# First entry of a fused attention and two-layer kernel: maxima and sums taken by TensorE, fewer whole products, another planned order

## The chip, the cores and the metric

One core of a Trainium2 chip runs one program. The metric is device time in microseconds (us). Three runs of the kernel before gave a median of 721.77 us, from 721.12 to 722.47 us. One more execution was profiled. Its engines are TensorE (PE for products and PEld for loads of the stationary operand), VectorE (DVE), ScalarE (ACT), GpSimd (POOL) and SyncE (SP), whose queue issues almost all transfers.

## What is computed

An attention between tokens and states runs first, and its rows then go through two feed-forward layers with different activations.

```python
def _attn_ref(x, state):                 # x (4, 8, 512, 64), state (4, 8, 32, 64)
    scores = scale * np.matmul(x, state.transpose(0, 1, 3, 2))
    scores = scores - scores.max(-1, keepdims=True)
    a = np.exp(scores)
    a /= a.sum(-1, keepdims=True) + 1e-09
    xread = np.matmul(a, state)          # tokens read states
    ...                                  # sread: states read tokens, the same way
    return np.concatenate([xread, sread], axis=2)

def _moe_ref(x, w_in, w_out):            # (2176, 512) -> 2048 -> 512
    h = x @ w_in
    g = np.where(h > 0.0, h, np.exp(np.minimum(h, 0.0)) - 1.0)
    return g @ w_out
def _moe2_ref(x, w_in, w_out):           # the same with h * tanh(log1p(exp(h)))
    ...
```

All inputs of the attention are float32, the weights float64 (read as pairs of 32-bit words and turned into float32 by ACT and DVE).

## The kernel before

**Blocks and steps.** The tokens of one batch entry are a block of 512 (blocks 0 to 3), and the 128 state rows are a small block of their own. The token part never forms `xread`: for each block the states are multiplied into the first weights (`fold`, PE line L574, result `m`), so that the first product of a step, `mm1`, is `m` times the probabilities `x`. The first layer is a list of steps (block, chunk j of 128 hidden columns): `mm1` gives `h`, `hidden` makes `g` from it on ACT and DVE (exp L806, relu L807, DVE L811 or L814), and two steps later `mm2` adds `g` times a row chunk of `w_out` into four accumulators (`acc`). Block 0 runs its chunks 0 to 7 first, then block 1 its chunks 0 to 7, then the second halves of both, then blocks 2 and 3.

**Whole and split products.** Most products are split: an operand is a high and a low part in the rounded type fp32r (copy on ACT, difference on DVE), and one product is three matmuls of 512 columns (L848, L849, L850). A whole product is one float32 matmul, which the trace shows as two records (L782 for `h`, L841 for `acc`). `whole_out` makes the second products of block 0 whole for chunks below `WHOLE_OUT = 6`; their `g` isn't split (L811), and the weight is split only after the step.

**First entry.** Block 0's probabilities are made at the program's start by `token_reads`, for two halves of four heads (`hf` 0 and 1). The x tiles are turned on PE (L641), scores come from 16 products on 64x32 pieces of the array (L653) with the states on partitions; then DVE turns each 32x32 square (L660) so that tokens are on partitions, takes the maximum over 32 states (L671), subtracts it (L672), ACT takes exp (L674), DVE sums (L675), adds eps (L676), takes the reciprocal (L677), multiplies (L678) and turns back (L680) into `x`. Ahead of that PE does ten turns of the identity (`warm`, L370), which wait until DVE has made it. The states of all four entries are loaded by two transfers of ACT's queue (L398).

**What sets the order.** Every operation is put into a `Plan` with a cost, its tiles and a due time, worked back from a table of step times; `run` is a list scheduler that takes, again and again, the operation that can start first (then the one due first) on any engine, and writes the instructions in that order. Each engine then executes its own list strictly in order. The two PSUM banks with the tag `att` are shared by folds, turns, scores and state reads.

## Time and profile before

| | |
|---|---|
| median of 3 runs | 721.77 us (721.12 to 722.47) |
| profiled execution, its own time | 722.41 us |
| its span, first to last instruction | 720.5 us |
| PE busy | 701.7 us, 97% of the span |
| DVE busy | 556.7 us, 77% |
| ACT busy | 495.8 us, 69% |
| granted TensorE clock, mean | 0.993 |

Busy time of PE counts overlapping records once, and a matmul's record reaches past the start of the next one; so the start-to-start spacing of records, and not their length, is what a product costs in a full stream. [...] A line number is that of the kernel before unless another is said.

### The profile page before, as it was taken

What the parts mean: (1) busy time and instruction counts of PE and PEld (TensorE: products, weight loads), DVE (VectorE), ACT (ScalarE), POOL (GpSimd) and SP (SyncE); (2) the same over time, 40 slices, a digit from 0 to 9 for tenths busy, and PEclk for the clock granted to TensorE, in tenths of its full rate; (3) what the DMA queues carried; (4) which work ended last, traced back from release to release, by engine and by line L of the source; (5) the groups of instructions that cost most, each with busy time, mean ns of one, the idle gap of its engine ahead of it and who ended that gap; (6) DMA issues with size and microseconds to landing.
All of it is one profiled execution on the core that took longest, in us unless ns stands there. A gap on an engine that the chain in (4) does not pass through costs nothing.

```text
span 720.5 us, 10191 instructions
## 1 busy us (share of the span) xinstructions
PE 701.7 (97%) x3698; PEld 546.3 (76%) x3698; DVE 556.7 (77%) x949; ACT 495.8 (69%) x861; POOL 3.0 (0%) x14
## 2 busy tenths in 40 slices
PE   5899999999989999999999999999999999999997
PEld 3345777777757778978887888878888888888886
DVE  6899988869879985447889998769738887767622
ACT  4797999768778776467868786669347666666522
POOL 0000000000000000000000000000000000000000
PEclk9799999999999999999999999999999999999999
DMA  9965556773685647106486454642035444401001
GB/s 224 276 180 138 128 174 227 234 234 99 209 258 167 200 146 246 51 20 229 164 279 225 150 147 127 221 163 58 1 117 147 136 127 125 142 27 58 15 1 58
DMA packets 65717, 106.83 MB, mean 148 GB/s; under 512 B 6660, under 2 KB 45572, under 8 KB 65668
## 3 DMA queue, kind: packets, MB, share of 16 engines
q1 hardware_dynamic: 63444, 105.53, 47.8%
q10 hardware_dynamic: 2224, 0.66, 0.4%
q8 instruction: 29, 0.48, 0.3%
q14 instruction: 20, 0.16, 0.1%
HBM read 78.38 MB, written 27.79 MB: 147 GB/s over the span
## 4 chain that ended last, share of the span: by engine, by line
PE 90%; DVE 7%; ACT 1%; issue 0%; DVEq 0%; ACTq 0%
PE prod L1018 20%; PE acc_acc L848 7%; PE acc_acc L850 7%; PE acc_acc L849 7%; PE accB L1057 4%; PE accB L1059 4%; PE accB L1058 4%; PE accA L1057 4%; PE accA L1059 4%; PE accA L1058 4%; PE h L791 3%; PE h L793 3%; PE h L792 3%; PE fold L574 2%; PE h L772 2%; PE acc_acc L841 2%
## 5 line engine op out<-in xcount | busy, mean ns | idle before, releaser
L1018 PE MATMUL prod<-x_t,pair 128*128 128x512 f32 x384 | 96.9, 390 | 0.5 <-ACT u__0_1_832_3916 L1044 0.5
L848 PE MATMUL acc_acc<-g,w_out 128*128 128x512 f32 x232 | 93.1, 401 | 0.0
L850 PE MATMUL acc_acc<-g,w_out 128*128 128x512 f32 x232 | 90.5, 390 | 0.0
L849 PE MATMUL acc_acc<-g,w_out 128*128 128x512 f32 x232 | 90.4, 390 | 0.0
L1018 PEld LDWEIGHTS prod<-x_t,pair 128*128 128x128 f32 x384 | 71.6, 188 | 15.5 <-ACT u__0_1_832_3916 L1044 1.0
L1018 PE MATMUL prod<-x_b,pair 128*128 128x512 f32 x288 | 72.4, 389 | 0.0
L976 ACT ACTIVATE e<-u,two 128x512 f32<-128x512 f32 x68 | 48.7, 722 | 21.7 <-DVE u L975 21.6
L1018 PEld LDWEIGHTS prod<-x_b,pair 128*128 128x128 f32 x288 | 54.1, 188 | 11.2
L814 DVE SCALAR_TENSOR_TENSOR e<-e,h 128x512 f32<-128x512 f32 x62 | 42.3, 683 | 25.5 <-ACT e L807 25.0
L806 ACT ACTIVATE e<-h 128x512 f32<-128x512 f32 x68 | 40.3, 595 | 26.2 <-PE h L793 17.3
L848 PEld LDWEIGHTS acc_acc<-g,w_out 128*128 128x128 f32 x232 | 43.7, 188 | 16.2 <-issue 5.4
L817 ACT CAST g<-e 128x512 fp32r<-128x512 f32 x62 | 38.4, 621 | 25.5 <-PE acc_acc L850 19.8
L978 DVE TENSOR_TENSOR u<-u,e 128x512 f32<-128x512 f32 x68 | 46.2, 687 | 12.0 <-ACT e L977 11.8
L818 DVE TENSOR_TENSOR g<-e,g 128x512 fp32r<-128x512 f32 x62 | 42.4, 685 | 14.6 <-ACT g L817 14.0
L850 PEld LDWEIGHTS acc_acc<-g,w_out 128*128 128x128 f32 x232 | 43.5, 188 | 9.3
L807 ACT ACTIVATE e<-e,one 128x512 f32<-128x512 f32 x68 | 49.2, 725 | 1.5
L1057 PE MATMUL accB<-w_out,g 128*128 128x512 f32 x128 | 50.0, 390 | 0.0
L849 PEld LDWEIGHTS acc_acc<-g,w_out 128*128 128x128 f32 x232 | 43.6, 188 | 8.4
L1059 PE MATMUL accB<-w_out,g 128*128 128x512 f32 x128 | 49.9, 390 | 0.0
L1058 PE MATMUL accA<-w_out,g 128*128 128x512 f32 x128 | 49.8, 389 | 0.0
L1059 PE MATMUL accA<-w_out,g 128*128 128x512 f32 x128 | 49.8, 389 | 0.0
L1058 PE MATMUL accB<-w_out,g 128*128 128x512 f32 x128 | 49.8, 389 | 0.0
(300 smaller groups left out, 1472.5 us busy)
## 6 DMA issues: line engine op xcount, KB each, us to landing
pair<-wi2d SPq DMA_DIRECT2D x64, 512.0 KB, 4.0
raw_out<-in_moe_w_out SPq DMA_DIRECT2D x32, 512.0 KB, 4.4
wi2d<-comb SPq DMA_DIRECT2D x64, 256.0 KB, 2.9
raw_in<-in_moe_w_in SPq DMA_DIRECT2D x32, 256.0 KB, 5.7
raw_in<-in_moe_w_in SPq DMA_DIRECT2D x16, 512.0 KB, 4.4
xb<-in_x SPq DMA_DIRECT2D x16, 256.0 KB, 4.9
x2d<-o SPq DMA_DIRECT2D x16, 256.0 KB, 3.9
out<-o SPq DMA_DIRECT2D x13, 256.0 KB, 2.5
```

Of the source, the lines that this page charges most:

```text
L807: add("ACT", act(n) + 0.12, lambda: nc.scalar.activation(E(), E(), AF.Relu, bias=one, scale=-1.0), r=[e, "one"], w=[e])
L814: add("DVE", dve(n), lambda: nc.vector.scalar_tensor_tensor(E(), E(), -1.0, Hh(), ALU.mult, ALU.max), r=[e, h], w=[e])
L818: add("DVE", dve(n), lambda: nc.vector.tensor_tensor(g[:, 1, :n], E(), g[:, 0, :n].bitcast(F32), ALU.subtract), r=[e, (g, 0)], w=[(g, 1)])
L848: nc.tensor.matmul(acc.t, lhsT=st[:, 0, :], rhs=mv[:, 0, :], start=fst, stop=False)
L849: nc.tensor.matmul(acc.t, lhsT=st[:, 0, :], rhs=mv[:, 1, :], start=False, stop=False)
L850: nc.tensor.matmul(acc.t, lhsT=st[:, 1, :], rhs=mv[:, 0, :], start=False, stop=lst)
L976: add("ACT", act(S) + 0.12, lambda: nc.scalar.activation(e.t, u.t, AF.Ln, bias=two), r=[u, "two"], w=[e])
L978: add("DVE", 0.69, lambda: nc.vector.tensor_tensor(u.t, u.t, e.t, ALU.mult), r=[u, e], w=[u])
L1018: nc.tensor.matmul(bank.t, lhsT=w[:, pos, a, c], rhs=x[b][:, k, :], start=first and k == i == 0, stop=k == 1 and i == 2, skip_group_check= ...
L1057: nc.tensor.matmul(acc.t, lhsT=g[:, 0, cols], rhs=w[:, 0, :], start=fst, stop=False)
L1058: nc.tensor.matmul(acc.t, lhsT=g[:, 0, cols], rhs=w[:, 1, :], start=False, stop=False)
L1059: nc.tensor.matmul(acc.t, lhsT=g[:, 1, cols], rhs=w[:, 0, :], start=False, stop=lst)
```

## The change

Five things are changed.

1. **Split products in block 0.** `WHOLE_OUT` goes from 6 to 2: the second products of chunks 2 to 5 of block 0 become split ones. Their `g` and weights are split before them.
2. **First entry.** `token_reads` no longer serves block 0; a new `first_reads` does. Scores stay with the states on partitions. PE turns them (`to_tokens`), DVE takes the maxima from the turned copy in PSUM, PE adds the negative maxima back into the scores' bank by products of a widened column with the identity (`take_top`), ACT takes exp from PSUM, PE sums over the 32 states by a product with a 0/1 matrix `heads` (`add_up`), DVE adds eps and takes the reciprocal of 8 columns, PE widens it (`spread`), and DVE multiplies once into `x`. `take_top` and `spread` are eight products each, on 128x32 pieces of the array.
3. **Opening products.** `warm` becomes nine products of a zeroed tile `blank`, filled by POOL, in place of ten turns of the identity.
4. **State loads.** ACT's queue loads block 0's states alone (two transfers of 64 KB); the rest goes by SP's queue.
5. **Order.** The planner charges entering and leaving the small-piece products (`mode`), has another time until which PE is costed as slow, and shifts the due times of randomly drawn operations by the 36 seeds of `MOVES`. The order changes on every engine, all through the program.

```diff
+INTO, OUT_OF = 0.09, 0.2
+MOVES = ((22389, 28.7), (74724, 6.4), ..., (67886, 555.8), (31972, 622.6), (92438, 638.2))
...
+            if e == "PE":
+                if t < COLD_UNTIL:
+                    c *= COLD
+                if op.mode != mode:
+                    c += INTO if op.mode else OUT_OF
+                    mode = op.mode
...
+    def shifts(self, moves):
+        shift = {}
+        for seed, a in moves:
+            rng = random.Random(seed)
+            span, sd, share = rng.choice((6, 15, 30)), rng.choice((1, 3, 8, 20)), rng.choice((0.02, 0.1, 0.3))
+            for op in self.ops:
+                if a <= op.due < a + span and rng.random() < share:
+                    shift[op.seq] = shift.get(op.seq, 0.0) + rng.gauss(0, sd)
+        return shift
...
-        add("PE", 0.24 * WARM, lambda: turns(pt, WARM), r=["ident"], w=[pt], due=-40.0)
+        add("POOL", 0.2, lambda: nc.gpsimd.memset(blank, 0.0), w=["blank"], due=-60.0)
+
+        def turns():
+            for i in range(WARM):
+                nc.tensor.matmul(pt[:, i % 4 * P:(i % 4 + 1) * P], lhsT=blank, rhs=blank, start=True, stop=True)
+
+        add("PE", 0.22 * WARM, turns, r=["blank"], w=[pt], due=-40.0)
...
         for i in range(2):
-            A(ACTQ, 256.0, lambda i=i: nc.scalar.dma_start(
-                out=raw[:, :, i, :], in_=state.rearrange("b (g h) n d -> (h n) (b g) d", g=2)),
-              w=[(raw, i)], due=-50.0)
+            A(ACTQ, 64.0, lambda i=i: nc.scalar.dma_start(out=raw[:, 0:2, i, :], in_=rows[:, 0:2]),
+              w=[(raw, 0, i)], due=-50.0)
+        for i in range(2):
+            A(SP, 192.0, lambda i=i: nc.sync.dma_start(out=raw[:, 2:, i, :], in_=rows[:, 2:]),
+              w=[(raw, 1, i)], due=STATES_DUE)
...
+    def first_reads(hf):
...
+        A("PE", 0.45, score_tiles, mode=1, r=[(xT, 0), (xT, 1), ("sd", 0)], w=ps)
+        turned = bank("turned", "h")
+        for t in range(2):
+            bk = ps[t]
...
+            A("ACT", act(2 * P), lambda t=t, bk=bk: copy("ACT", raw[:, hf, t, :], bk[:, 0:2 * P]),
+              r=[bk], w=[(raw, hf, t)], place=[mx, sm, turned])
+
+            def to_tokens(t=t):
+                for c in range(2):
+                    nc.tensor.transpose(turned[:, (2 * t + c) * P:(2 * t + c + 1) * P], raw[:, hf, t, c * P:(c + 1) * P], ident)
+
+            A("PE", 0.25, to_tokens, r=["ident", (raw, hf, t)], w=[(turned, t)])
+            A("DVE", 0.43, lambda t=t, mx=mx: nc.vector.tensor_reduce(
+                mx.t, turned[:, t * 2 * P:(t + 1) * 2 * P].rearrange("p (c h n) -> p c h n", c=2, n=NS), AX.X, ALU.max, negate=True),
+              r=[(turned, t)], w=[mx])
+
+            def take_top(bk=bk, mx=mx):
+                for c, h, l in heads_of:
+                    nc.tensor.matmul(bk[l, c * P:(c + 1) * P], lhsT=wide(mx, c, h), rhs=ident, start=False, stop=True,
+                                     skip_group_check=True, tile_position=(0, h * NS))
+
+            A("PE", 0.45, take_top, mode=1, r=["ident", mx], w=[bk])
+            A("ACT", act(2 * P), lambda t=t, bk=bk: nc.scalar.activation(
+                ex[:, hf, t, :], bk[:, 0:2 * P], AF.Exp, scale=SCALE), r=[bk], w=[(ex, hf, t)])
+
+            def add_up(t=t, bk=bk):
+                for c in range(2):
+                    nc.tensor.matmul(bk[:, 2 * P + c * HH:2 * P + (c + 1) * HH], lhsT=ex[:, hf, t, c * P:(c + 1) * P],
+                                     rhs=heads, start=True, stop=True)
+
+            A("PE", 0.45, add_up, r=["heads", (ex, hf, t)], w=[bk])
+            A("DVE", 0.17, lambda bk=bk, sm=sm: nc.vector.tensor_scalar(
+                sm.t, bk[:, 2 * P:2 * P + 2 * HH].rearrange("p (c h) -> p c h", c=2), EPS, None, ALU.add), r=[bk], w=[sm])
+            A("DVE", 0.25, lambda sm=sm: nc.vector.reciprocal(sm.t, sm.t), r=[sm], w=[sm])
+
+            def spread(bk=bk, sm=sm):
+                for c, h, l in heads_of:
+                    nc.tensor.matmul(bk[l, half(c)], lhsT=wide(sm, c, h), rhs=ident, start=True, stop=True,
+                                     tile_position=(0, h * NS))
+
+            A("PE", 0.45, spread, mode=1, r=["ident", sm], w=[bk])
+            A("DVE", 0.43, lambda t=t, bk=bk: nc.vector.tensor_tensor(
+                xt[:, hf, :].rearrange("p (c t f) -> p t c f", c=2, t=2)[:, t],
+                ex[:, hf, t, :].rearrange("p (c f) -> p c f", c=2),
+                bk[:, 2 * P:].rearrange("p (c f) -> p c f", c=2), ALU.mult), r=[bk, (ex, hf, t)], w=[(xt, hf, t)])
...
-READY_AT, COLD_UNTIL, COLD = 0.75, 16.0, 1.35
+READY_AT, COLD_UNTIL, COLD = 0.75, 5.0, 1.95
-WHOLE_OUT = 6
+STATES_DUE = 20.0
+WHOLE_OUT = 2
-WARM, EARLY, XB, EBUFS, GBUFS, FOLD_LAG = 10, 8, 3, 2, 2, 5.0
+WARM, EARLY, XB, EBUFS, GBUFS, FOLD_LAG = 9, 8, 3, 2, 2, 5.0
```

What moves is shown at three places. The first is DVE in the first entry. Before, its list holds the turned probabilities (`prob`), the maxima (`mx`) and, between them, the words of the first weights (`wv`, `w`).

```order
L660 STREAM_TRANSPOSE prob_159<-scores_157 128x256
L660 STREAM_TRANSPOSE prob_159<-scores_158 128x256
L671 TENSOR_REDUCE mx_161<-prob_159 128x16
L672 TENSOR_TENSOR prob_159<-prob_159,mx_161 128x512
L299 COPY sd_79<-st_184 128x256
L660 STREAM_TRANSPOSE prob_196<-scores_194 128x256
L466 SCALAR_TENSOR_TENSOR wv_192<-wy_191,wv_192 128x512
```

After the change (line numbers of the new kernel) the four maxima stand in a row, and sums and the one multiplication into `x` come between the same weight words.

```order
L705 TENSOR_REDUCE top_177<-turned_179 128x8
L705 TENSOR_REDUCE top_181<-turned_179 128x8
L705 TENSOR_REDUCE top_225<-turned_227 128x8
L705 TENSOR_REDUCE top_229<-turned_227 128x8
L724 TENSOR_SCALAR sum_178<-scores_161 128x8
L726 RECIPROCAL sum_178<-sum_178 128x8
L516 SCALAR_TENSOR_TENSOR wv_204<-wy_203,wv_204 128x512
L724 TENSOR_SCALAR sum_182<-scores_160 128x8
L528 SCALAR_TENSOR_TENSOR w_0_33_272<-wy_203,wv_204 128x4x128
L726 RECIPROCAL sum_182<-sum_182 128x8
L734 TENSOR_TENSOR x_0_4_289<-ex_6_234,scores_161 128x2x128
```

Per group of 256 columns the list has four operations of DVE where it had most of eight, and none of them is wider than 256 columns.

The second place is ACT ahead of the exp of block 0's seventh step, chunk 6 (its `h` is `h_211` before, `h_214` after). Before:

```order
L461 ACTIVATE wy_523<-raw_out_7_79_464 128x512
L299 CAST x1hl_528<-x_0_6_270 128x512
L463 ACTIVATE wv_524<-raw_out_7_79_464 128x512
L299 CAST w_out_6_75_539<-wv_503 128x512
L299 COPY xT_532<-xT_541 128x512
L299 CAST x1hl_528<-x_0_6_270 128x512
L461 ACTIVATE wy_557<-raw_in_8_83_497 128x512
L806 ACTIVATE e_575<-h_211_550 128x512
```

After:

```order
L511 ACTIVATE wy_693<-raw_out_7_84_617 128x512
L341 COPY m_1_153_491<-fold_683 128x256
L341 COPY m_1_153_491<-fold_682 128x256
L513 ACTIVATE wv_694<-raw_out_7_84_617 128x512
L341 CAST x1hl_586<-x_0_4_289 128x512
L341 CAST w_out_6_80_721<-wv_673 128x512
L341 CAST x_1_159_706<-pT_719 128x512
L917 ACTIVATE e_741<-h_214_713 128x512
```

The exp stands at row 74 of ACT's list before and at row 86 after: folded weights, block 1's probabilities (`x_1`) and, further up, four copies of `g` now come ahead of it.

The third place is PE in the middle of block 2, where block 3's x tiles are turned (`xT`) behind its scores. Before:

```order
L653 MATMUL scores_2251<-xT_2221,sd_80 32x256
L653 MATMUL scores_2252<-xT_2221,sd_80 32x256
L641 MATMUL xT_2268<-ident,xb_2069 128x128 x4
L641 MATMUL xT_2275<-ident,xb_2069 128x128 x4
L848 MATMUL acc_2_acc_535_2283<-g_2036,w_out_0_193_390 128x512
```

After:

```order
L772 MATMUL scores_2538<-xT_2505,sd_82 32x256
L902 MATMUL h_607_2551<-x_2_294_1909,m_8_0_473_2412 128x512
L903 MATMUL h_607_2551<-x_2_294_1909,m_8_0_473_2412 128x512
L904 MATMUL h_607_2551<-x_2_294_1909,m_8_1_474_2413 128x512
L760 MATMUL xT_2560<-ident,xb_2261 128x128 x4
L760 MATMUL xT_2568<-ident,xb_2261 128x128 x4
L902 MATMUL h_607_2551<-x_2_294_1909,m_8_0_473_2412 128x512
```

Three products of `h` now stand between the scores and the turns, which need the banks that the scores and the folds fill.

## Rows read from the trace of the kernel before

**Rows 1.** The page: busy time by engine, and the chain that ended last.
```profile
PE 701.7 (97%) x3698; PEld 546.3 (76%) x3698; DVE 556.7 (77%) x949; ACT 495.8 (69%) x861; POOL 3.0 (0%) x14
...
PE 90%; DVE 7%; ACT 1%; issue 0%; DVEq 0%; ACTq 0%
```

**Rows 2.** Busy by stretch: PE, PEld, DVE, ACT, POOL (records), granted clock, DMA share, GB/s.
```profile
10.00:15.00 5.00, 1.82 (x22) 0.68 (x20) 4.08 (x9) 3.80 (x9) 0.00 (x0) 1.00 1.13 222
15.00:20.00 5.00, 1.85 (x32) 0.62 (x32) 5.00 (x12) 4.51 (x12) 0.00 (x0) 0.54 1.10 263
...
25.00:30.00 5.00, 5.00 (x39) 1.41 (x39) 3.33 (x6) 4.76 (x9) 0.00 (x0) 0.93 1.07 298
```

**Rows 3.** The same view of one long stretch.
```profile
25.50:120.00 94.50, 93.08 (x516) 56.91 (x515) 87.32 (x151) 84.51 (x156) 1.58 (x4) 1.00 0.63 180
```

**Rows 4.** Timeline of PE: start, duration, line, tiles, records, idle before and releaser.
```profile
3.12 2.39 PE L370 MATMUL warm<-ident 128*128 128x128 f32 x10 [3.12 <-DVE ident L356]
5.30 1.92 PE L641 MATMUL xT<-ident,xb 128*128 128x128 f32 x8
...
10.01 0.60 PE L411 MATMUL st<-ident,st_raw 128*128 128x128 f32 x4
...
15.31 0.49 PE L574 MATMUL fold<-w,sd 64*32 64x128 f32 x2 [3.32 <-DVE w L478]
...
20.36 2.08 PE L782 MATMUL h<-x,m 128*128 128x512 f32 x2 [1.17 <-DVE x L680]
22.86 3.37 PE L782 MATMUL h<-x,m 128*128 128x512 f32 x4 [0.42 <-DVE x L680]
26.15 0.66 PE L574 MATMUL fold<-w,sd 64*32 64x256 f32 x16
```

**Rows 5.** Timeline of DVE in the first entry.
```profile
9.68 0.45 DVE L660 STREAM_TRANSPOSE prob<-scores 128x256 f32<-128x256 f32 x1
...
11.33 0.69 DVE L671 TENSOR_REDUCE mx<-prob 128x16 f32<-128x512 f32 x1
...
17.55 0.25 DVE L677 RECIPROCAL sm<-sm 128x16 f32<-128x16 f32 x1
...
22.10 0.70 DVE L680 STREAM_TRANSPOSE x<-prob 128x512 f32<-128x512 f32 x1
```

**Rows 6.** Timeline of PE among the second products of block 0.
```profile
47.67 3.60 PE L841 MATMUL acc_acc<-gw,whole 128*128 128x512 f32 x8
51.11 1.04 PE L641 MATMUL xT<-ident,xb 128*128 128x128 f32 x8
...
64.80 0.50 PE L848 MATMUL acc_acc<-g,w_out 128*128 128x512 f32 x1
```

**Rows 7.** Timeline of PE around the products of one state read.
```profile
77.75 0.40 PE L792 MATMUL h<-x,m 128*128 128x512 f32 x1
77.98 0.40 PE L793 MATMUL h<-x,m 128*128 128x512 f32 x1
78.31 0.66 PE L724 MATMUL sr<-xb,exT 128*32 128x64 f32 x32
78.90 0.50 PE L848 MATMUL acc_acc<-g,w_out 128*128 128x512 f32 x1
```

**Rows 8.** Timeline of PE where block 3's x tiles are turned.
```profile
204.40 1.25 PE L641 MATMUL xT<-ident,xb 128*128 128x128 f32 x8 [1.46 <-DVE m L588]
...
208.36 0.87 PE L641 MATMUL xT<-ident,xb 128*128 128x128 f32 x6 [0.52 <-ACT raw L299]
```

**Rows 9.** Time to landing: the last first-entry x transfer (issued 2.23), then raw_out's first (9.81).
```profile
DMA to landing us min/median/max: 5.8/6.1/6.3
...
DMA to landing us min/median/max: 9.7/9.7/9.7
```

**Rows 10.** ACT: the first weight word of raw_out, and busy times to the seventh step's relu.
```profile
23.46 0.67 ACT L461 ACTIVATE wy<-raw_out 128x512 f32<-128x512 f32 x1 [3.21 <-issue]
...
0.00:55.25 55.25, 44.93 (x248) 20.78 (x248) 44.97 (x89) 39.24 (x75) 0.31 (x6) 0.91 0.90 226
```

## The prediction

> **What bounds the kernel now.** I read the page first. PE is busy 97% of the span and holds 90% of the chain that ended last [rows 1], so time is won where PE has less to do, waits less, or starts its stream sooner. Then the busy times by stretch: PE works 1.8 of 5 us in each of the two stretches from 10 to 20, and 5.0 of 5 from 25 on [rows 2]; the start is the one place where it waits much. The timeline says for whom: the first product of `h` comes at 20.36 and the second pair at 22.86, both released by DVE's last turn of the probabilities (L680) [rows 4]. DVE is full there, 5.00 of 5 us between 15 and 20 [rows 2]. From 25.5 to 120 PE is idle for 1.4 of 94.5 us, and DVE (87.3) and ACT (84.5) are nearly as full [rows 3]: what PE gains in that stretch, those two must be able to follow.

> The profiled execution took 722.41 us, 1.9 more than its span of 720.5, and 0.64 more than the median of 721.77. I sum against it and take 0.64 off at the end.

> **Split for whole products.** Eight records of a whole product, four products, take from 47.67 to 51.11, so 0.86 each [rows 6]. A split one is three matmuls 0.23 apart [rows 7], 0.69. Four steps of four products: 16 x 0.17 = **-2.7 us** of PE. The price is four more differences of `g` on DVE and four more copies on ACT, and weights split earlier; it lies beside PE's work and is met below.

> **First entry.** Before, the third product of `h` is done when the fold begins at 26.15 [rows 4]. I work out when it is done after.

> *Opening.* PE waits 3.12 us for the identity and then turns ten tiles [rows 4]. `blank` needs only POOL, so PE starts near 1.0. A product of 128 columns costs between 0.21 (a turn: the eight of x start about 0.21 apart) and 0.43 (a quarter of the whole product's 0.86, doubled for the slow clock); I take 0.43, the same kind of matmul, and the nine end at 4.9. Turns of x follow as tiles land. Block 0's states are now a quarter of what ran beside x, so the last x tile, landed at 8.5 before (2.23 + 6.3) [rows 9], comes near 7.3. The remaining states go by SP ahead of the fourth weight; the bytes up to raw_out's first tile (landed at 19.5) [rows 9] are the same.

> *Chain.* Scores of the first half run near 7.7, those of the second near 9.6. Copies of `raw`, turns and maxima (half of L671's 0.69 each [rows 5], taken as 0.4) put the first `take_top` at 10.2. Its eight products of 128 columns have no row of their own. Bounds: 0.43, if four pieces overlap perfectly, and 8 x 0.215 = 1.7 if none do. The nearest row is the state read, 16 products of half as many columns on pieces of the same shape in 0.66 [rows 7]; I take 0.6. `add_up` is two products of 4 columns, between 0.05 and 0.4; I take 0.3. DVE's eps and reciprocal cost at most 0.25 each (L677), the last multiplication 0.45 as the turn of 256 columns (L660) [rows 5]. ACT's exps stand in line behind weight words: the second half's first exp waits behind three, until 13.9. On DVE two words stand between sum and reciprocal of each later group. Followed through the new lists, `x` of the first half is ready at 17.2 and of the second at 19.8, against 20.3 and 22.8 (L680's end [rows 5]). DVE spends 4 x 1.35 = 5.4 us on it; before, each half had two turns of 0.45, four operations like L671's 0.69, two small ones and one of 0.70 [rows 5], 4.8 us, or 9.6 for both. PE's own additions, some 6 us, fall into 10 to 20, where it was idle for 6.3 of 10 us [rows 2].

> *Products and clock.* [...] The third ends at 22.1: **-4.0 us**. Ends: -5.0 (second half's `x` 1 us sooner), and -0.5 with the clock down and pieces that don't overlap.

> [...] The eight turns of x at 5.30 start some 0.21 apart and the four of the states at 10.01 only 0.11 apart [rows 4], though PE had done nothing but turns from 3.12 to 8.9: turns did bring the clock up. [...]

> **Following PE from 25 to 120.** PE needs 94.5 - 2.7 - 1.4 (its idle time) + 0.6 (below) = 91.0 us for this stretch. By the lists, from the first step's `g` (or relu) to that of the same later step, DVE has 149 instructions where it had 147 and ACT 145 where it had 142, some 1.2 us more each: DVE 88.5 us, 97% of 91.0, against 92% before. ACT has slack to draw on: raw_out's first tile landed at 19.5, and ACT took it up at 23.46 after 3.21 us of idling [rows 9, 10], because the two word buffers waited for DVE, which was busy with the first entry. I let PE wait 1.5 us in this stretch where it waited 1.4; the ends are 0 and 4.8.

> **Other waits.** Two waits at 204.40 and 208.36, 2.0 us together, come from turns that stand right behind a fold and behind scores and need their banks [rows 8]. In the new list three products (0.7 us) stand between scores and turns, and the fold is further off: **-2.0 us**, ends 0 and -2.0. So waits give -1.4 + 1.5 - 2.0 = **-1.9**. The rest I leave alone.

> **Entering and leaving small pieces.** A group of piece products costs 0.10 to enter (0.33 instead of 0.23 from the record ahead) and 0.10 to leave (0.50 long instead of 0.40) [rows 7]. Behind the first entry the new list has 34 such groups, the old 30: 4 x 0.2 = **+0.8 us**.

> **Sum.** -2.7 - 4.0 - 1.9 + 0.8 = -7.8: 714.6 for the profiled execution, 714.0 for the median.

> **The rivals.**

> *DVE can't follow (0.20).* If DVE is no better used than before, 92%, its 88.5 us take 95.8, and PE waits 4.8 instead of 1.5: 717.3. For it: DVE fed by ACT through two buffers waits now and then at 92%. Against: with less in the first entry, both start the stretch ahead.

> *The clock falls in the first entry (0.15).* Products on 32-column pieces may not hold it: between 16 and 19 folds of that kind ran at 0.54 [rows 2] and did not raise it. Three products at half rate cost 2.5 more, and part of that returns as waits that fall away: 714.0 + 2.0 = 716.0.

> *Pieces don't overlap (0.05), so the first entry doesn't do what it is for.* Four of the eight calls lie on the chain, 1.1 us more each: 718.4.

> *Better (0.17).* The new order clears the 1.5 us of waits, and the first entry ends a microsecond sooner: 711.5.

> *Slower: ACT's list ahead of the seventh step (0.05).* Before that step's exp ACT now has some 6.4 us more (four copies of `g`, four more of `raw`, folded weights, block 1's probabilities). Before, the relu behind it ended at 55.25 with 39.24 us of work [rows 10], so 16.0 idle, and the second product ran at 64.80 [rows 6]. With 45.6 of work and the same idle time it ends at 61.6; another 2.8 (DVE, ACT and DVE again) lead to 64.4. The rest of PE's list behind that product is about 5 us shorter than it was. The kernel becomes slower, above 723.2, if ACT idles some 7 us longer than before ahead of this exp, waiting in order on words whose tiles haven't landed or whose buffers are taken. I expect it to idle less.

> **How the numbers follow.** The forecast of 714.0 has 0.38, with its own range 712 to 716. The range of 8 in 10 leaves out part of the better case below and of the worst two above: 710.0 to 718.5. A measurement of this kernel can tell about 0.2%, 1.4 us, from no change. Slower by more than that is the last rival, 0.05; within it, when two of the rivals meet, 0.04; faster 0.91.

> **What would show it.** Right: PE begins before 1.5; the third L893 record pair ends near 22; the granted clock is 1.00 in 10 to 25; `take_top` and `spread` take 0.5 to 0.8 each; PE's idle time from 25 to 112 is 1 to 3 us; no wait at block 3's turns; 32 fewer L841-kind records and 48 more split ones. Wrong: a granted clock near 0.5 between 15 and 25 (second rival), PE idle above 4 us between 25 and 112 with DVE near 92% (first), calls of 1.5 us (third), ACT idle above 20 us ahead of the seventh step's exp (last).

## The result, and the profile after

The changed kernel takes 710.80 us (median of 4 runs, 710.24 to 711.56) where the kernel before took 721.44 (4 runs of the same sitting). The ratio is 0.9851, with a 95% interval from 0.9834 to 0.9868: 10.6 us less. The forecast was 714.0 in a range from 710.0 to 718.5, so the time lies in the range and the gain was foreseen too small. The profiled execution took 710.84 us with a span of 709.0, 11.5 less than the span before.

The page after, to be read beside [rows 1]: busy time by engine, and the chain that ended last.

```profile
PE 702.3 (99%) x3874; PEld 555.5 (78%) x3874; DVE 551.1 (78%) x945; ACT 497.1 (70%) x873; POOL 2.8 (0%) x20
...
PE 97%; DMA 1%; SPq 1%; DVE 0%; ACT 0%; issue 0%; ACTq 0%
```

PE's busy time is hardly changed (702.3 against 701.7), though the split products take less of it: the first entry has more, smaller products. The 11.5 us are time in which PE did nothing before. The next view lists all that PE still waits for in the whole program (us in total, times, longest).

```profile
PE h L893 <- DVE sum L726: 1.0, 1, 1.0
PE warm L424 <- POOL one L401: 1.0, 1, 1.0
PE scores L720 <- ACT ex L715: 0.2, 1, 0.2
```

All three lie in the first 18 us. The same view of before has thirteen lines. Those whose waits lie behind the first entry and last longest are:

```profile
PE xT L641 <- DVE m L588: 1.5, 1, 1.5
PE h L791 <- ACT x L299: 0.8, 1, 0.8
PE turn L1219 <- DVE g L987: 0.6, 1, 0.6
PE prod L1018 <- ACT u__0_1_832_3916 L1044: 0.5, 1, 0.5
```

Busy times of after by stretch, for [rows 2] and [rows 3]: PE, PEld, DVE, ACT, POOL (records), granted clock (a share of full speed), DMA share, GB/s.

```profile
10.00:15.00 5.00, 5.00 (x112) 3.85 (x104) 3.81 (x12) 4.07 (x11) 0.00 (x0) 1.00 1.23 215
15.00:20.00 5.00, 3.70 (x41) 1.86 (x42) 2.17 (x7) 1.89 (x7) 0.00 (x0) 0.79 1.07 288
20.00:25.00 5.00, 5.00 (x52) 2.60 (x44) 3.25 (x8) 3.74 (x8) 0.00 (x0) 0.87 1.13 222
25.00:30.00 5.00, 5.00 (x27) 1.81 (x26) 4.93 (x9) 4.89 (x10) 0.00 (x0) 1.00 1.10 249
...
25.50:120.00 94.50, 94.50 (x584) 64.00 (x584) 88.40 (x155) 86.71 (x162) 1.12 (x4) 1.00 0.64 183
```

Two things stand out. From 25.5 to 120 PE is never idle, with DVE at 88.4 and ACT at 86.7 of 94.5 us. And between 15 and 25 the granted clock does fall, less than before but by enough to be seen. The timeline of PE shows where (start, duration, line, tiles, records, idle before and releaser; answers to [rows 4]).

```profile
0.98 3.83 PE L424 MATMUL warm<-blank 128*128 128x128 f32 x18 [0.98 <-POOL one L401]
...
12.01 0.64 PE L711 MATMUL scores<-ident,top 128*32 128x128 f32 x16
12.47 0.62 PE L730 MATMUL scores<-ident,sum 128*32 128x128 f32 x16
...
17.55 1.75 PE L893 MATMUL h<-x,m 128*128 128x512 f32 x2 [0.99 <-DVE sum L726]
19.22 1.94 PE L730 MATMUL scores<-ident,sum 128*32 128x128 f32 x32
21.09 0.97 PE L462 MATMUL st<-ident,st_raw 128*128 128x128 f32 x6
21.89 1.88 PE L893 MATMUL h<-x,m 128*128 128x512 f32 x4
23.71 0.74 PE L625 MATMUL fold<-w,sd 64*32 64x256 f32 x16
```

The first product of `h` waits 0.99 us and takes 1.75 instead of 1.12; the two calls of `spread` behind it take 1.94 together where one takes 0.62 at 12.47. The third product is done at 23.7. It was 26.15 before, and 22.1 was predicted.

### The profile page after: what moved, and what is told of

Same layout as the page of the kernel before. It is cut to its first block, busy times and chain, and to the rows that moved or that the text cites. A ratio compares the mean times of both kernels' runs of the same rounds, so it can differ in the third digit from the quotient of the medians.

```text
span 709.0 us, 10553 instructions
## 1 busy us (share of the span) xinstructions
PE 702.3 (99%) x3874; PEld 555.5 (78%) x3874; DVE 551.1 (78%) x945; ACT 497.1 (70%) x873; POOL 2.8 (0%) x20
## 4 chain that ended last, share of the span: by engine, by line
PE 97%; DMA 1%; SPq 1%; DVE 0%; ACT 0%; issue 0%; ACTq 0%
PE prod L1129 22%; PE acc_acc L959 8%; PE acc_acc L961 8%; PE acc_acc L960 8%; PE accA L1168 4%; PE accB L1170 4%; PE accA L1170 4%; PE accA L1169 4%; PE accB L1169 4%; PE accB L1168 4%; PE h L902 4%; PE h L904 4%; PE h L903 4%; PE fold L625 2%; PE h L893 2%; PE h L883 2%
## 5 line engine op out<-in xcount | busy, mean ns | idle before, releaser
L959 PE MATMUL acc_acc<-g,w_out 128*128 128x512 f32 x248 | 100.6, 406 | 0.0
L961 PE MATMUL acc_acc<-g,w_out 128*128 128x512 f32 x248 | 97.0, 391 | 0.0
L960 PE MATMUL acc_acc<-g,w_out 128*128 128x512 f32 x248 | 96.7, 390 | 0.0
L959 PEld LDWEIGHTS acc_acc<-g,w_out 128*128 128x128 f32 x248 | 46.6, 188 | 18.7 <-issue 5.7
L925 DVE SCALAR_TENSOR_TENSOR e<-e,h 128x512 f32<-128x512 f32 x66 | 45.1, 683 | 20.3 <-ACT e L918 20.2
L928 ACT CAST g<-e 128x512 fp32r<-128x512 f32 x66 | 40.8, 619 | 24.7 <-PE acc_acc L961 16.6
L1089 DVE TENSOR_TENSOR u<-u,e 128x512 f32<-128x512 f32 x68 | 46.5, 688 | 14.2 <-ACT e L1088 13.9
L961 PEld LDWEIGHTS acc_acc<-g,w_out 128*128 128x128 f32 x248 | 46.5, 188 | 10.2
L960 PEld LDWEIGHTS acc_acc<-g,w_out 128*128 128x128 f32 x248 | 46.6, 188 | 9.2 <-issue 0.5
L929 DVE TENSOR_TENSOR g<-e,g 128x512 fp32r<-128x512 f32 x66 | 45.2, 686 | 10.3 <-ACT g L928 9.8
L1168 PE MATMUL accA<-w_out,g 128*128 128x512 f32 x128 | 50.0, 391 | 0.0
L1169 PE MATMUL accA<-w_out,g 128*128 128x512 f32 x128 | 49.8, 389 | 0.0
L1170 PE MATMUL accA<-w_out,g 128*128 128x512 f32 x128 | 49.8, 389 | 0.0
```

The costliest lines, as they stand in the source:

```text
L925: add("DVE", dve(n), lambda: nc.vector.scalar_tensor_tensor(E(), E(), -1.0, Hh(), ALU.mult, ALU.max), r=[e, h], w=[e])
L929: add("DVE", dve(n), lambda: nc.vector.tensor_tensor(g[:, 1, :n], E(), g[:, 0, :n].bitcast(F32), ALU.subtract), r=[e, (g, 0)], w=[(g, 1)])
L959: nc.tensor.matmul(acc.t, lhsT=st[:, 0, :], rhs=mv[:, 0, :], start=fst, stop=False)
L960: nc.tensor.matmul(acc.t, lhsT=st[:, 0, :], rhs=mv[:, 1, :], start=False, stop=False)
L961: nc.tensor.matmul(acc.t, lhsT=st[:, 1, :], rhs=mv[:, 0, :], start=False, stop=lst)
L1089: add("DVE", 0.69, lambda: nc.vector.tensor_tensor(u.t, u.t, e.t, ALU.mult), r=[u, e], w=[u])
```

## The experiments

All but those with fewer seeds or none were built in one way: the planner was run first without writing anything, its order was taken down, and the program was written in that order with one edit, or with two where that is said. Every engine's list is then that of after but for the edit. A time "by the ratios" compares the ratios to the kernel before, each from its own sitting. (Line numbers in these kernels are shifted by the inserted lines.)

### What the seeded order is worth

```diff
-MOVES = ((22389, 28.7), (74724, 6.4), ..., (92438, 638.2))
+MOVES = ()
```

> The changed kernel with an empty list of seeds: the planner works with its plain due times, everything else as after. Theory 1 (the seeded order took the waits away): PE waits again behind the first entry, 3 to 6 us in all between 25 and 700, where after waits 0 and before waited 4.8; time 714 to 717. Theory 2 (the shorter first entry and the smaller load did it, whatever the order): PE idles under 1 us there and the time is 710 to 712.

Measured: 731.33 us, ratio 1.0131 to before [1.0116, 1.0146]. Without its seeds the changed kernel is **slower than before**, and 20.5 us slower than after; both theories had the loss far too small. Busy times by stretch and PE's longest wait:

```profile
25.00:113.00 88.00, 79.07 (x445) 51.72 (x446) 82.67 (x147) 72.71 (x131) 1.51 (x4) 0.94 0.62 173
113.00:325.00 212.00, 210.18 (x1340) 162.31 (x1339) 163.50 (x292) 154.48 (x275) 0.83 (x4) 1.00 0.54 172
325.00:690.00 365.00, 362.57 (x1654) 298.19 (x1653) 288.77 (x463) 246.62 (x412) 0.00 (x0) 1.00 0.40 132
...
77.02 0.79 PE L902 MATMUL h<-x,m 128*128 128x512 f32 x1 [7.05 <-ACT x L341]
```

PE is idle for 8.9, 1.8 and 2.4 us in the three stretches, 13.2 in all, where after has none. Behind a single wait of 7.05 us, for block 1's probabilities, the clock is down as well (0.94 over the first stretch): the records start 0.43 apart and not 0.23, up to 83.7, which costs some 3 us more. The waits are a matter of the order: theory 1 holds in kind, theory 2 is dead. No run gave the kernel before a seeded order of its own, so how much of the 10.6 us the seeds alone would bring there stays open.

```diff
-MOVES = ((22389, 28.7), ..., (5708, 26.2), (46971, 38.8), (96447, 63.6), ...)
+MOVES = ((46971, 38.8), (96447, 63.6), ...)
```

> The changed kernel without the ten seeds whose stretch of due times begins below 30; the 26 later ones stay. Theory 1 in the form that the late shifts clear the late waits: PE idles under 1 us behind 120, and what is lost is in the first 120 us: 711 to 714. Theory 1 in the form that all seeds were fitted to one another: the later waits return too, 714 to 717. Theory 2 (order does not matter): 710 to 712.

Measured: 727.66 us, ratio 1.0080 [1.0065, 1.0095]. PE is idle 5.4 us from 25 to 113, but also 3.0 and 1.5 in the two stretches behind, though the seeds for these were kept: a changed start upsets what was fitted to it. This is the second form of theory 1, at a size that it did not expect (714 to 717).

```diff
-MOVES = ((22389, 28.7), ...)
-WHOLE_OUT = 2
+MOVES = ()
+WHOLE_OUT = 6
```

> The changed kernel without seeds and with six whole chunks in block 0 again: the new first entry alone, in the order of the planner's plain due times. If the loss without seeds (731.3) is a matter of the order alone, this loses too: 726 to 736, with PE idle 5 us or more behind the first entry. If the four chunks more of split products are what the plain order can't carry on DVE and ACT: most of the waits go and the time is 717 to 723.

Measured: 730.26 us, ratio 1.0105 [1.0087, 1.0124]. The new first entry without the four additional split chunks, in the planner's plain order, loses as well, with waits in quite other places (PE idle 2.2, 3.2 and 5.1 us in the three stretches). So it is not the four additional split chunks that the plain order can't carry.

### Split for whole, by itself

```diff
+                if kind and not blk and WHOLE_OUT <= j < 6:
+                    nc.tensor.matmul(acc.t, lhsT=st[:, 0, :].bitcast(F32), rhs=mv[:, 0, :].bitcast(F32), start=fst, stop=lst)
+                    return
```

> The changed kernel, its order of every engine kept instruction by instruction; only the 16 second products of block 0's chunks 2 to 5 are one whole float32 matmul on the high parts instead of three split ones (the products with the low parts are left out). Theory 1 (PE is the limit there, so the split gives its full size): 16 x 0.17 = 2.7 us more than after, about 713.5. Theory 2 (DVE and ACT, 92% busy each between 21 and 113, set the pace there): PE waits less in exchange, and the time rises by less than 1 us, to 711.8 at most.

Measured: 713.87 us, ratio 0.9888 [0.9872, 0.9905] against 0.9851 of after: 2.7 us more by the ratios, 3.1 by the medians, where theory 1 said 2.7. Part of that need not be the edit's, since the first entries differ too. The same two calls in the profiled executions, the product of `h` behind the fourth folds and a later fold, in after and in this kernel:

```profile
24.38 1.13 PE L893 MATMUL h<-x,m 128*128 128x512 f32 x2
60.47 1.09 PE L625 MATMUL fold<-w,sd 64*32 64x512 f32 x16
...
26.46 1.13 PE L908 MATMUL h<-x,m 128*128 128x512 f32 x2
65.25 1.09 PE L640 MATMUL fold<-w,sd 64*32 64x512 f32 x16
```

The first of them comes 2.08 us later here (PE stands for 1.49 us, and the mean granted clock is 0.995 against 0.996), which the edit doesn't touch. From there to the fold, where the edited products lie, another 2.70 us are lost (4.78 in all), as theory 1 said. PE is busy 88.00 of 88.00 us from 25 to 113 in this kernel too: what a product costs there goes into the time in full.

### Can DVE follow

```diff
+            out.append((Extra, "DVE"))
...
+    Extra.fn = lambda: nc.vector.tensor_tensor(blank, ident, ident, ALU.mult)
```

> The changed kernel in its own order, with one extra DVE operation (a 128x128 product of the identity with itself into the blank tile, about 0.2 us) behind each of the first 22 splits of g: about 4.4 us more of DVE between 25 and 115, so DVE is busy some 97% there, as the prediction had it. By the prediction's term (1.5 us of waits at 97%): 712.3. By its first rival (DVE is never better used than the 92% it showed): 4 us more, 715. If the list has slack at the places that matter: within 0.5 of after, 711.3 at most.

Measured: 711.97 us, ratio 0.9865 [0.9850, 0.9879]: 1.0 us more than after by the ratios, with intervals that overlap. The stretch from 25 to 113, and the added group (busy in total, mean ns):

```profile
25.00:113.00 88.00, 87.79 (x511) 58.70 (x510) 84.05 (x158) 81.44 (x151) 1.66 (x4) 1.00 0.64 182
...
L91 DVE TENSOR_TENSOR blank<-ident 128x128 f32<-128x128 f32 x22 | 6.2, 283 | 0.0
```

DVE is busy 84.05 of 88 us, 95.5%, so the first rival of the prediction (DVE is never better used than 92%) is wrong. The time lies between the last expectation (711.3 at most) and the prediction's term (712.3). PE is idle for only 0.21 us, but that view hides short waits, since a record reaches past the start of the next one (0.40 long at a spacing of 0.23 [rows 7]). The same PE work, from the product of `h` behind the fourth folds to one state read, in after and in this kernel:

```profile
24.38:112.41 88.03, 88.03 (x518) 58.99 (x512) 81.95 (x142) 82.38 (x154) 1.12 (x4) 1.00 0.64 181
...
23.89:113.26 89.37, 89.16 (x519) 59.05 (x513) 85.24 (x160) 82.67 (x153) 1.66 (x4) 1.00 0.65 182
```

It takes 1.34 us longer with DVE at 95.4%. So DVE can follow at that load, at a price near the prediction's 1.5 us and not within the list's slack; in after itself DVE is at 93.1% of this stretch, and the load of 97% didn't arise.

### Why the first entry gained less than predicted

```diff
 MATMUL fold<-w,sd  x8
-MATMUL h<-x,m 128x512
 MATMUL scores<-ident,sum 32x128 x8     (spread, twice)
 MATMUL scores<-ident,sum 32x128 x8
+MATMUL h<-x,m 128x512
```

> The changed kernel in its own order but for one place on PE: the two last calls of `spread` stand ahead of the first product of h and not behind it. If the order of these three is what cost the first entry its missing 1.5 us (third product done at 23.7 where 22.1 was predicted): the last x is ready near 19 and the third product done near 22.3, 1.4 us less than after, about 709.4. If the fallen clock is the cause (0.50 from 18 to 21): the third product is done at 23 or later and the gain is under 0.7 us, 710.1 to 710.8.

Measured: 710.83 us, ratio 0.9851 [0.9837, 0.9865], exactly as after.

```profile
17.72 1.08 PE L748 MATMUL scores<-ident,sum 128*32 128x128 f32 x32 [0.95 <-DVE w L546]
...
22.66 1.33 PE L643 MATMUL fold<-w,sd 64*32 64x256 f32 x16 [0.43 <-DVE w L546]
```

The third product is done at 22.2 here, as hoped, and then little comes of it: the folds of the fourth chunk wait for DVE's last word (`w`) of the fourth weight tile. The clock stayed at 1.00.

```diff
-            for i in range(WARM):
-                nc.tensor.matmul(pt[:, i % 4 * P:(i % 4 + 1) * P], lhsT=blank, rhs=blank, start=True, stop=True)
+            for i in range(10):
+                nc.tensor.transpose(pt[:, i % 4 * P:(i % 4 + 1) * P], ident, ident)
```

> The changed kernel in its own order, but PE opens with ten turns of the identity, which it must wait for, in place of nine blank products. If the blank products bring the clock up and the chain forward, as charged: PE starts at 3.1, the first scores come 0.5 to 1 us later and the time is 0.5 to 1 us longer, 711.3 to 711.8. [...] If the chain waits for the x tiles anyway and turns bring the clock up as before: as after, 710.5 to 711.1.

Measured: 710.56 us, ratio 0.9848 [0.9834, 0.9861]: no difference from after.

```profile
5.33 0.98 PE L689 MATMUL xT<-ident,xb 128*128 128x128 f32 x4
6.14 0.38 PE L478 MATMUL st<-ident,st_raw 128*128 128x128 f32 x2
6.36 1.38 PE L689 MATMUL xT<-ident,xb 128*128 128x128 f32 x8
...
16.80 1.13 PE L909 MATMUL h<-x,m 128*128 128x512 f32 x2
...
22.59 1.32 PE L641 MATMUL fold<-w,sd 64*32 64x256 f32 x16 [1.14 <-DVE w L544]
23.85 1.12 PE L909 MATMUL h<-x,m 128*128 128x512 f32 x2
```

The opening of blank products brings nothing here: PE begins at 3.14 instead of 0.98, but the x tiles set the pace. The turns get faster behind turns alone: four take 0.81 us from 5.33 to 6.14, the next two 0.22. The clock is 1.00 from there to 30. The first product of `h` even comes sooner, without any wait, and PE then stands for 1.14 us at the same folds. In these two kernels, and at 22.64 in the one with more DVE work, the folds start within 0.1 us of each other however early PE was. So these folds start at 22.6 at best, by the fourth tile and not by the chain of the probabilities. They then take 1.3 us instead of 0.74, with DVE still copying the other states (`sd`) up to 23.1, and the product of `h` behind them starts at 23.85 where after has it at 24.38. These 0.53 us are all that was left to gain here, and they are kept to the end: the span is 708.4 against 709.0. The tile is behind the rest of the states on SP's queue; ACT of after idles for it:

```profile
19.60 0.67 ACT L511 ACTIVATE wy<-raw_in 128x512 f32<-128x512 f32 x1 [2.53 <-DMA raw_in<-in_moe_w_in]
```

Two runs tried to loosen that.

```diff
 DMA raw_in_2 x2
-DMA st_raw<-in_state 128x6x64 x2
 DMA raw_in_3 x2
+DMA st_raw<-in_state 128x6x64 x2
```

> The changed kernel in its own order but for this: the SP queue issues the fourth tile of first weights ahead of the rest of the states (two transfers of 192 KB), and the turns of these states on PE, with one copy on ACT, stand behind the second and third product of h instead of ahead of them. Theory A (the first entry ends with that tile: in four runs the folds of the fourth chunk start at 22.6, released by DVE's word of it, however early PE was): the tile lands 1.5 to 2.5 us sooner, the folds start near 21.3, and the time is 1.0 to 1.4 us shorter than after, 709.4 to 709.8. Theory B (what PE gains there it gives back between 25 and 113, where DVE and ACT are over 90% busy): the folds start sooner, PE waits later by as much, and the time is 710.4 to 711.0.

Measured: 712.93 us, ratio 0.9868 [0.9855, 0.9881]: 1.2 us more than after by the ratios, so neither theory's time, with intervals that overlap; in the trace the product of `h` behind the fourth folds starts at 26.71, 2.33 later. The tile landed at 16.65 instead of 19.5, but the turns of the states that the edit moved behind `h` then stood ahead of the folds, which waited 0.30 us for `sd` besides, and the wait ahead of the first product of `h` was 1.83 us. Whether the landing could be turned into time by a better place for the turns stays open.

```diff
-dma_start(out=raw[:, 0:2, i, :], in_=rows[:, 0:2])      (ACT's queue)
-dma_start(out=raw[:, 2:, i, :], in_=rows[:, 2:])        (SP's queue)
+dma_start(out=raw[:, :, i, :], in_=rows)                (ACT's queue)
```

> The changed kernel in its own order, but the states of all four entries come by two transfers of ACT's queue at the start, as before, and the SP queue loads none. The x tiles share their time with four times the bytes and land up to 1.6 us later; the fourth tile of first weights lands about 1 us sooner. By theory A the later x tiles cost nothing as long as the chain still ends ahead of 22: 709.8 to 710.8. If the chain from the x tiles sets the end: the first product of h comes 1 to 1.5 us later and the time is 711.5 to 712.5.

Measured: 713.57 us, ratio 0.9875 [0.9861, 0.9888]: 1.7 us more than after by the ratios, as the second branch said, though the intervals just overlap. PE's wait for the states:

```profile
7.53 0.41 PE L477 MATMUL st<-ident,st_raw 128*128 128x128 f32 x2 [2.07 <-DMA st_raw<-in_state]
```

It holds up the whole chain: the first product of `h` comes at 21.34, 3.8 us later, and the folds start at 27.50. The smaller state load is a real part of the gain, which the prediction had not priced by itself.

### What PE waits for ahead of the first product of `h`

```diff
 MATMUL fold<-w,sd  x8
+MATMUL scores<-blank 128x128 x4
 MATMUL h<-x,m 128x512
```

> The changed kernel in its own order, with four products of the blank tile on PE just ahead of the first product of h, where PE waits 0.99 us (they write columns of a scores bank that nobody reads any more). If the clock falls because PE waits there: the granted clock stays at 1.00 from 15 to 25, the first product of h takes 1.1 us instead of 1.75 and the two calls of `spread` 1.1 instead of 1.94; 0.8 to 1.5 us less than after, 709.3 to 710.0. If the fall has another reason (small pieces that do not count): the clock still falls and the time is as after or up to 0.3 longer, 710.8 to 711.1.

Measured: 712.08 us, ratio 0.9869 [0.9847, 0.9891], runs from 710.29 to 714.51: too scattered to tell from after. The trace says more.

```profile
16.32 0.62 PE L655 MATMUL fold<-w,sd 64*32 64x128 f32 x16
17.67 2.03 PE L91 MATMUL scores<-blank 128*128 128x128 f32 x8 [0.73 <-issue]
```

The blank products, which need nothing new, wait themselves: the wait is that of a *place* in PE's list and not of `h`, and the profile names no releaser for it. The clock falls to 0.50 from 18 to 21 here too.

The edits of this run and of the one with `spread` first, together:

> Both edits at once: four blank products where PE waits, then the two last calls of `spread`, then the first product of h. If order and clock each have their own share: third product of h done near 22.0, 708.8 to 709.4. If they are one and the same cause: no better than the better of the two alone.

Measured: 710.95 us, ratio 0.9849 [0.9836, 0.9862], as after. The blank products take 1.1 us themselves, so the folds start at 23.08, now without a wait, where `spread` first alone had them at 22.66.

Counting settles it. The trace has 220 product records of PE ahead of the wait in after (a float32 product leaves two, a turn one), and 220 in each of the ten kernels above that show such a wait: seven in the order of after, and the three with fewer seeds or none, whose order is another and whose wait stands ahead of a fold (0.90 us up to 18.05 without seeds). The opening of ten turns has 8 records fewer than that of nine blank products (10 for 18). There the wait should move 8 records down the list. In the run above with that opening no wait is seen at all: PE gets to the place only at 18.0.

```diff
-DMA st_raw<-in_state 128x6x64 x2                     (the edit of the run with the tile first)
+DMA st_raw<-in_state 128x6x64 x2
-MATMUL warm<-blank 128x128 x9
+MATMUL warm<-ident 128x128 x10
```

> The changed kernel in its own order with two edits: the fourth tile of first weights ahead of the rest of the states, as in the run of that name, and ten turns of the identity as opening, which is 16 instructions fewer on PE's list (20 instead of 36) ahead of the first product of h. In the run with the tile first, PE stood still for 1.83 us ahead of that product although all it reads was there; in every run a 16 KB packet of instructions starts some 2.6 to 3.2 us before PE goes on. Theory F (PE waits there for the supply of its own instructions): with 16 fewer the place of the wait moves past the product, PE waits there less than 0.3 us, the folds of the fourth chunk start near 22 and the time is 709.0 to 710.0. Theory D (a tile or bank that the trace does not name): the wait of 1 us or more stays ahead of the first product of h, the clock falls again and the time is 711.5 to 713.

Measured: 712.13 us, ratio 0.9874 [0.9856, 0.9892], so not the time that theory F gave (the moved turns cost here too). Its wait does what F said:

```profile
17.75 1.13 PE L928 MATMUL h<-x,m 128*128 128x512 f32 x2
18.80 0.42 PE L765 MATMUL scores<-ident,sum 128*32 128x128 f32 x6
19.98 1.03 PE L765 MATMUL scores<-ident,sum 128*32 128x128 f32 x26 [0.76 <-issue]
```

The product of `h` runs without waiting (with the other opening it waited 1.83), and PE stops in the middle of a call of `spread`, whose eight products read one tile that is long there: behind 2 + 6 = 8 further records, again after the 220th. No tile or bank can do that; theory D falls.

## Why the prediction came out

**Split products: right.** Predicted -2.7 of PE in full, measured 2.7 to 3.1 in the run that puts the whole products back, and 2.7 in its trace where the products lie. Of the list of what would show it, 48 records of whole products have become 16, and each split line has 248 where it had 232.

**First entry: right in kind, too large.** Predicted -4.0, measured -2.4 (26.15 to 23.71). The chain itself was ahead of the forecast: `take_top` and `spread` take 0.64 and 0.62 a call (0.6), and with ten turns as opening the first product of `h` ran at 16.80, near the 17.2 predicted. Two steps failed. The first is "the bytes up to raw_out's first tile are the same": the term followed PE, DVE and ACT, and not the fourth weight tile. By three runs the folds that need it start at 22.6 at best, and the product of `h` behind them at 23.85, against 26.75 before: -2.9 was the most there was. The second is the end of the third product at 22.1, which has the three products at full clock. The profiled execution doesn't show that term: it has 23.71, at clocks of 0.79 and 0.87, while the run with `spread` first has 22.2, at 1.00. Up to 17.5 PE's list has 220 product records where it had 82, and behind the 220th PE stops once, for 0.3 to 2.1 us by run, as it seems for the supply of its instructions, for which the trace of before had no row. With that stop the second rival came true for some 3 us of the profiled execution (clock 0.79 and 0.87); with the wait it costs 0.5 us (24.38 against 23.85), since in the runs with the clock at 1.00 the folds wait for the tile instead.

**Waits: the step that was furthest off.** Predicted -1.9, measured -4.8: idle time of PE in the stretches 25 to 113, 113 to 325 and 325 to 690 goes from 1.42, 2.24 and 1.13 us to nothing. Two sentences failed. "I let PE wait 1.5 us" from 25 to 120, since DVE would be 97% busy: DVE is busy 88.40 of 94.50 us, 93.5%, and PE waits 0. The price itself was about right, as the run with more DVE work shows (1.34 us at 95.4%); the load that it was put on did not come. "The rest I leave alone" kept three smaller waits behind 120, of 0.3 to 0.6 us, that [rows 8] don't show (at 242.96, 382.03 and 661.74 before); the new order cleared them too. The two waits that the lists did show were judged rightly.

**Small pieces:** +0.8 was not measured by itself.

Together: -2.7 - 2.4 - 4.8 + 0.8 = -9.1 of the 11.5 that the span lost. Most of the rest is an effect of the view: a split product's record is 0.40 long at a spacing of 0.23 [rows 7], so each wait hides 0.17 us behind the record ahead of it; for eight waits behind 25 that makes an estimated 1.4. The last 1.0 stays open.

So the two errors cancelled in part, 1.6 too much in the first entry and 2.9 too little in the waits; as far as they did, the forecast was near by luck. **The rivals:** that DVE can't follow is refuted; the clock fell for a short time (0.50 from 18 to 21) at little cost (0.5 us); the pieces overlap, as calls of 0.62 to 0.64 show. ACT's list ahead of the seventh step did not hold anything up: that exp starts at 55.30, released by its own product, and ACT had idled 13.0 us by then (42.33 busy), less than the 16.0 before.

```profile
55.30 0.60 ACT L917 ACTIVATE e<-h 128x512 f32<-128x512 f32 x1 [0.28 <-PE h L893]
```

"Better", at 711.5, was nearest, for one of its two reasons: the waits were cleared, but the first entry was not sooner.

What the prediction could not know is how much hung on the seeds. It read the new order at three places and took it as given, which was enough for the sign. The runs without seeds show the other side: with the same work in the plain order the kernel is 1.3% slower than before.

## What to carry to other kernels

With PE 97% busy, the remaining waits of this kernel were a property of the order as a whole. Remove work only together with a new fit of the order, and test each part in the order that will run, because a part tried in an unfitted order shows the loss of the order and not its own gain. For a chain that is made shorter, look up what else must arrive by its new end, weight tiles on the same queue above all, before charging its full length. Where a stretch is cut into many small instructions, count them: here their supply seems to have stopped PE for up to 2.08 us. And where records overlap (here 0.40 long at a spacing of 0.23), a busy share of 100% doesn't show that nothing waited; compare when the same instruction starts in two traces.

## What the hardware showed

```profile
q8 instruction: 30, 0.49, 0.3%
...
q8 instruction: 1, 0.02, 81.6%
```

A packet is 0.49 MB / 30 = 16 KB, and PE's 3874 records of products and 3874 of loads make 258 for each of the 30; before there were 29. The wait ends 2.6 to 3.2 us after a packet starts in each of these six kernels:

| kernel | packet starts | PE goes on | it waited |
|---|---|---|---|
| after | 14.6 | 17.55 | 0.99 |
| more DVE work | 14.8 | 17.51 | 0.28 |
| whole products back | 15.3 | 18.52 | 1.49 |
| tile first | 15.4 | 18.39 | 1.83 |
| states by ACT's queue | 18.7 | 21.34 | 2.08 |
| tile first, ten turns | 17.3 | 19.98 | 0.76 |

The place in the list is shown by the counts of 220; that the packets hold PE's instructions, and that this one is what PE waits for, is inferred from counts and times. It fits that the run with ten turns and nothing else doesn't wait: its packet starts at 14.8, and PE gets to the place 3.2 us later.

**In these runs turns alone brought the clock up.** With ten turns as the opening, turns start 0.20 apart from 5.33 and 0.11 apart from 6.14, with nothing but turns ahead, as [rows 4] had suggested. With blank products the same step, from 0.21 apart to 0.11, comes at 4.3. That the step is the clock's is read from the spacing: the view by stretch doesn't show it, since it has 1.00 for any time ahead of the clock's first change too (in after also from 2 to 4, where the products start 0.21 apart).

**How long PE waited did not by itself decide whether the clock fell.** After 0.99 us it fell to 0.50 from 18 to 21, and after 0.73 with the four blank products likewise; after 0.95 with `spread` first it stayed at 1.00, and so it did after 1.60 with the late seeds alone.

```profile
18.32 0.45 PE L625 MATMUL fold<-w,sd 64*32 64x128 f32 x16 [1.60 <-issue]
```

What decides was not tried.
